# Three chunks of 512 rows and one of 256 in layer two of an attention, expert and MLP kernel

## The chip, the cores and the metric

The kernel runs on one core of a Trainium2 chip, in one launch. The metric is the device time of one execution in microseconds; the median of three runs is given. The profile is of one further execution.

## The reference

Three parts run one after the other. An attention with a small state gives 2176 rows of 512 features. A mixture of experts sends each row to one of eight experts (two matrices with a relu between them) and scales the result. Layer two, which the change is about, is a plain two-layer network over these rows:

```python
def _moe2(x, w_in, w_out):          # x [rows, 512], w_in [512, 2048], w_out [2048, 512]
    h = x @ w_in
    relu6 = np.clip(h + 3.0, 0.0, 6.0)
    g = h * relu6 / 6.0
    return (g @ w_out).astype(np.float32)
```

In the test the inputs are float32 or wider; the weights of layer two arrive as 64-bit floats.

## The kernel before, in words

The expert stage leaves its rows in `y_pad`, seven chunks of 256 rows (`NCS = 7`; the padded places scatter nowhere). Layer two starts from there. Every float32 product is made of three matmuls on a high and a low part of each operand: high by high, high by low, low by high. So `yTh`/`yTl` are the two parts of the turned rows, `wh`/`wl` of the weights, `gh`/`gl` of the hidden values.

The hidden dimension of 2048 is cut into 16 steps `m` of 128. A step of a chunk is:

- the first product, `mm3` (L1102): twelve matmuls into one PSUM tile `p3`, eight on `wh` and then four on `wl`, each streaming 256 columns of `yTh` or `yTl` (two pieces of 128);
- its activation: `u` on ScalarE (L1123), `g` on VectorE (L1124), the cast `gh` on ScalarE (L1125), and `gl = g - gh` on VectorE, or on GpSimd in the first group up to step 13 (L1126);
- the second product, `mm4` (L1129): per half of 128 rows three matmuls of 512 columns of `wh`/`wl` into an accumulator `po`, summed over the 16 steps.

TensorE runs one step ahead (`late`): first product of step m, then the second product of step m-1. Chunks 0 and 1 go together as the first group (`groups`, L1256), since the weights are converted only there; chunks 2 to 6 are groups of their own with all weights in SBUF. The accumulators `po` have four PSUM banks, two a chunk.

In the first group each step m also does the following. `advance` (L963) hands VectorE conversion instructions of the weights, 64-bit to float32, three an eighth of a matrix (L939, L941, L943; `NA = 2` behind each first product), and SP the loads into the two `st` tiles. `prep` (L947) makes `wh` on ScalarE (L957) and `wl` on GpSimd (L958) for step m+2. Steps 2, 4 and 6 fill the output with zeros.

The rows of the next group are fetched by `fetch` (L898): loads into two `yg` tiles at step 10, and at steps 12 and 14 one half each is split by `rest`: `fid` on VectorE, the cast `yTh` on ScalarE (L912), `yTl` on VectorE (L913). Three pairs of `yTh`/`yTl` tiles take turns (`c % 3`; the third lies in the pool `mw`). When a chunk's last second product is done, `put` (L1247) copies each half to a tile `o` (ScalarE L1252, VectorE L1250; four tiles) and GpSimd scatters it to the output (L1253); all scatters write `out_dram`, so each waits for the one before.

In the last chunk the steps from `16 - NH` on do only the first half of the second product; their `gh`/`gl` are held, and the other half follows at the end, so that the first half's scatter goes out while TensorE works on the second (L1294 to L1302). `NH = 7` is also the count of `gh`/`gl` tiles.

Expert pairs earlier in the kernel borrow SBUF tiles for their weights (`spare`, L1045), among them the four `yT` tiles. A loop at the end (L1351 on) serves overflowing experts; it is not entered with these inputs.

Of the kernel before, what the change touches and what calls it, by code (L numbers as in the profile page):

```python
# [595 lines left out]
def full(ctx, tc, x, state, w_gate, w1, w2, capacity, w_in, w_out, out, dbg=None):  # L596
# [448 lines left out]
    spare = [(vv, f"v{m}") for m in range(NV - NSP, NV)] + [(vv, "wh0"), (vv, "wl0")] + [(mk, f"yT{h}{t}") for t in range(2) for h in "hl"]  # L1045
    turn_of = [0]

    def p_loads(which, es_, ks=(0, 2, 1, 3)):
        raws = {}
        for k in ks:  # L1050
            for g in range(2):
                pool, tag = spare[turn_of[0] % len(spare)]
                turn_of[0] += 1
                raws[k, g] = load(which, es_[g], k, pool=pool, tag=tag, bufs=1)
# [343 lines left out]
```

## Time and profile before

| | us |
|---|---|
| median of three runs (575.43, 575.67, 579.76) | 575.67 |
| the profiled execution, its own time | 579.37 |
| its span from the first to the last instruction | 577.2 |
| TensorE busy in the span | 555.5 |
| VectorE, ScalarE, GpSimd busy | 307.5, 222.2, 141.9 |

Engines: PE is TensorE (matmuls), PEld its weight loads, DVE VectorE, ACT ScalarE, POOL GpSimd, SP the engine that issues most DMAs. A line such as L1111 is the line of the kernel whose instruction it is. The ends of matmuls are modelled, so the pace of a stretch is taken from starts: the start of the next matmul less the start of this one.

### The profile page before, as it was taken

How to read it: one execution, taken by the hardware profiler on the slowest of the kernel's cores; microseconds unless marked ns; L12 is line 12 of the kernel's file. 1: busy time of each engine (PE TensorE's matmuls, PEld its weight loads, DVE VectorE, ACT ScalarE, POOL GpSimd, SP SyncE). 2: the span in 40 equal slices, each digit the busy share in tenths (PEclk: the TensorE clock that was granted, in tenths of full speed). 3: DMA queues.
4: the chain of work that ended last, by engine and by line, in shares of the span. 5: the costliest groups of instructions: out<-in, count | busy, mean ns of one | idle time of the engine just before them, and what ended most of it. 6: DMA issues, size and time to landing. Idle time of an engine off the chain costs nothing.

```text
span 577.2 us, 10492 instructions
## 1 busy us (share of the span) xinstructions
PE 555.5 (96%) x3974; PEld 484.7 (84%) x3974; DVE 307.5 (53%) x700; ACT 222.2 (39%) x462; POOL 141.9 (25%) x195
## 2 busy tenths in 40 slices
PE   6998889899999999999999999999999999999996
PEld 3655789796969697899999888999999999999994
DVE  4888974437635674466769863333233333233331
ACT  4878621234304250325434543333334333333331
POOL 5435634201510110016676742001001001001001
PEclk9999889899999999999999999999999999999999
DMA  6735711896979793234863411001001001000000
GB/s 138 177 144 186 250 77 48 267 398 227 386 258 403 237 346 100 96 130 147 297 233 112 146 38 56 18 19 56 1 18 56 1 19 56 1 1 19 20 1 30
DMA packets 52201, 75.26 MB, mean 130 GB/s; under 512 B 23121, under 2 KB 31313, under 8 KB 51634
## 3 DMA queue, kind: packets, MB, share of 16 engines
q1 hardware_dynamic: 49634, 67.09, 34.7%
q0 software_dynamic: 2240, 7.38, 3.7%
q8 instruction: 33, 0.54, 0.4%
q14 instruction: 22, 0.18, 0.1%
q10 hardware_dynamic: 272, 0.07, 0.1%
HBM read 70.75 MB, written 16.49 MB: 151 GB/s over the span
## 4 chain that ended last, share of the span: by engine, by line
issue 36%; PE 29%; DMA 10%; DVE 5%; ACT 1%; POOL 0%; POOLq 0%; DVEq 0%; ACTq 0%
PE pm L798 10%; PE pm L809 10%; DMA out_dram<-o,fid 6%; PE pm L1086 2%; PE pm L1066 2%; DMA st<-in_moe_w_out_dram 2%; PE p L1111 2%; DVE v L943 2%; DMA st<-in_moe_w_in_dram 1%; DVE g L1124 1%; DVE v L939 1%; DVE v L941 1%; PE po L1134 1%; ACT wh L957 1%; PE pxt L764 1%
## 5 line engine op out<-in xcount | busy, mean ns | idle before, releaser
L1111 PE MATMUL p<-yTh,wh 128*128 128x256 f32 x448 | 110.5, 280 | 0.0
L1111 PE MATMUL p<-yTl,wh 128*128 128x256 f32 x448 | 110.5, 280 | 0.0
L1124 DVE SCALAR_TENSOR_TENSOR g<-u,p 128x256 f32<-128x256 f32 x110 | 46.1, 419 | 115.9 <-ACT u L1123 115.8
L1123 ACT ACTIVATE u<-p,b 128x256 f32<-128x256 f32 x110 | 52.0, 473 | 108.9 <-PE p L1111 108.9
L1111 PEld LDWEIGHTS p<-yTl,wh 128*128 128x128 f32 x448 | 84.5, 189 | 3.9
L1111 PEld LDWEIGHTS p<-yTh,wh 128*128 128x128 f32 x448 | 84.4, 188 | 3.8
L1134 PE MATMUL po<-wh,gh 128*128 128x512 f32 x220 | 86.3, 392 | 0.0
L1134 PE MATMUL po<-wh,gl 128*128 128x512 f32 x220 | 86.2, 392 | 0.0
L1134 PE MATMUL po<-wl,gh 128*128 128x512 f32 x220 | 86.1, 391 | 0.0
L1125 ACT CAST gh<-g 128x256 fp32r<-128x256 f32 x110 | 44.7, 406 | 80.7 <-DVE g L1124 80.7
L1111 PE MATMUL p<-yTh,wl 128*128 128x256 f32 x448 | 71.6, 282 | 0.9 <-POOL wl L958 0.9
L1253 POOL DMA_INDIRECT out_dram<-o,fid x14 | 13.9, 994 | 219.5 <-ACT o L1252 162.8
L1111 PEld LDWEIGHTS p<-yTh,wl 128*128 128x128 f32 x448 | 60.7, 189 | 1.7 <-POOL wl L958 1.7
L1126 DVE TENSOR_TENSOR gl<-g,gh 128x256 fp32r<-128x256 f32 x84 | 36.7, 437 | 39.8 <-ACT gh L1125 39.8
L1134 PEld LDWEIGHTS po<-wh,gl 128*128 128x128 f32 x220 | 41.3, 188 | 9.8 <-POOL gl L1126 0.4
L798 PE MATMUL pm<-xth,w1h 128*128 128x256 f32 x160 | 45.9, 291 | 1.4 <-DVE xb L813 1.4
L798 PE MATMUL pm<-xth,w1l 128*128 128x256 f32 x160 | 45.0, 285 | 1.3 <-DVEq L1156 1.3
L1134 PEld LDWEIGHTS po<-wh,gh 128*128 128x128 f32 x220 | 41.4, 188 | 5.2
L1134 PEld LDWEIGHTS po<-wl,gh 128*128 128x128 f32 x220 | 41.4, 188 | 5.2
L809 PE MATMUL pm<-hth,w2h 128*128 128x256 f32 x160 | 45.2, 282 | 0.0
L809 PE MATMUL pm<-htl,w2h 128*128 128x256 f32 x160 | 44.7, 280 | 0.0
L809 PE MATMUL pm<-hth,w2l 128*128 128x256 f32 x160 | 44.6, 278 | 0.0
(285 smaller groups left out, 1005.0 us busy)
## 6 DMA issues: line engine op xcount, KB each, us to landing
raw<-in_moe_w_dram SPq DMA_DIRECT2D x80, 512.0 KB
st<-in_moe_w_in_dram SPq DMA_DIRECT2D x16, 512.0 KB
st<-in_moe_w_out_dram SPq DMA_DIRECT2D x16, 512.0 KB
x_rows<-xrow SPq DMA_DIRECT2D x4, 1072.0 KB
xb<-in_x_dram SPq DMA_DIRECT2D x32, 128.0 KB
yg<-y_pad SPq DMA_DIRECT2D x14, 258.0 KB
out_dram<-zt SPq DMA_DIRECT2D x2, 1536.0 KB
y_pad<-y SPq DMA_DIRECT2D x5, 516.0 KB
```

The lines of the kernel that those rows point to most:

```text
L798: T.matmul(ps[:, j], W1[l][k][:, ls], xT[r][:, k], start=n == 0, stop=n == 11)
L809: T.matmul(ps[:, j], W2[l][k // 2][:, k % 2, ls], hT[k // 2][r][:, k % 2], start=k == 0 and i == 0, stop=k == 7 and i == 2)
L943: V.scalar_tensor_tensor(out=t, in0=lo, scalar=29, in1=t, op0=ALU.logical_shift_right, op1=ALU.bitwise_or)
L1066: T.matmul(ps[n][64 * g:64 * g + 64, :], th[:, 128 * k + 64 * g:128 * k + 64 * g + 64], raws[k, g][:, 512 * n:512 * n + 512], start=i == 0 ...
L1086: T.matmul(ps[64 * g:64 * g + 64, :], th[:, 128 * k + 64 * g:128 * k + 64 * g + 64], raws[k // 2, g][:, 512 * (k % 2):512 * (k % 2) + 512] ...
L1111: T.matmul(pv, l[:, 128 * k:128 * k + 128], r[:, :, 128 * k:128 * k + 128], start=n == 0, stop=n == 11)
L1123: A.activation(out=u, in_=ps, func=AF.Relu, bias=b3)
L1124: V.scalar_tensor_tensor(out=g, in0=u, scalar=6.0, in1=ps, op0=ALU.min, op1=ALU.mult)
L1125: A.copy(gh, g)
L1126: eng.tensor_tensor(out=gl, in0=g, in1=gh.bitcast(F32), op=ALU.subtract)
L1134: T.matmul(po[t], l[:, ls], r[:, 512:1024], start=m == 0 and i == 0, stop=m == 15 and i == 2)
L1253: G.indirect_dma_start(out=out, out_offset=bass.IndirectOffsetOnAxis(ap=fid[:, t:t + 1], axis=0), in_=o, in_offset=None, bounds_check=B * ...
```

## The change

Chunks 0 and 1, 2 and 3, 4 and 5 become three groups of 512 rows, chunk 6 stays alone. In a group of two chunks `mm3` makes one first product for both: twelve matmuls of 512 columns (four pieces of 128) into a full PSUM bank, and one `u`, `g`, `gh`, `gl` of 512 columns. `mm4` still goes chunk by chunk on halves of the wide `gh`/`gl`.

What follows from it: the `yT` tiles are twice as wide (`wide`, two sets in turn, one in `mk` and one in `mw`); `gh`/`gl` are three wide tiles each, so `NH` falls to 5; `u` has one tile, `o` three; two tiles of 16 columns (`pad0`, `pad1`) shift what is allocated behind them; the borrowed `yT` tiles of the expert pairs hold two raw weight tiles each. In the first group all four conversion instructions of a step stand behind the one first product (`advance(2 * NA)`). A group's two chunks are fetched at steps 8 and 12, and split at steps 10, 11 and 14, 15. The loop at the end is rewritten to use the wide tiles.

```diff
-NH = 7
+NH = 5
...
-    def fetch(at, slot=0):
-        pool = mw if slot == 2 else mk
-        yTh = pool.tile([128, 2, DM], F32R, name=f"yTh{slot}", bufs=1)
-        yTl = pool.tile([128, 2, DM], F32R, name=f"yTl{slot}", bufs=1)
+    def wide(slot):
+        pool = mw if slot else mk
+        return [pool.tile([128, 4, DM], F32R, name=f"yT{h}{slot}", bufs=1) for h in "hl"]
+
+    def fetch(at, y, half=0):
+        yTh, yTl = (v[:, 2 * half:2 * half + 2] for v in y)
...
-    def mm3(m, yTh, yTl, early=False, eng=V):
+    def mm3(m, y, n=4, early=False, eng=V, into=None):
...
-                    T.matmul(pv, l[:, 128 * k:128 * k + 128], r[:, :, 128 * k:128 * k + 128], start=n == 0, stop=n == 11)
+                    T.matmul(pv, l[:, 128 * k:128 * k + 128], r[:, 0:n, 128 * k:128 * k + 128], start=i == 0, stop=i == 11)
...
-            u = mw.tile([128, 256], F32, name="u", bufs=2)
-            g = mw.tile([128, 256], F32, name="g", bufs=2)
-            gh = mw.tile([128, 256], F32R, name="gh", bufs=NH)
-            gl = mw.tile([128, 256], F32R, name="gl", bufs=NH)
+            u = mw.tile([128, 512], F32, name="u", bufs=1)[:, 0:128 * n]
+            g = mw.tile([128, 512], F32, name="g", bufs=2)[:, 0:128 * n]
+            gh, gl = into or both()
...
+    def both():
+        if not padded:
+            first = [mw.tile([128, 512], F32R, name=f"g{h}", bufs=3) for h in "hl"]
+            padded.append(mw.tile([128, 16], F32, name="pad1"))
+            return first
+        return [mw.tile([128, 512], F32R, name=f"g{h}", bufs=3) for h in "hl"]
...
-    g0 = mm3(0, *ft[0][0][0:2], True)
-    g1 = mm3(0, *ft[1][0][0:2], True)
+    g01 = mm3(0, ys[0], early=True)
...
+    mw.tile([128, 16], F32, name="pad0")
+    ys[1] = wide(1)
...
-        o = mw.tile([128, DM], F32, name="o", bufs=4)
+        o = mw.tile([128, DM], F32, name="o", bufs=3)
...
-    groups = [(0, 1)] + [(c,) for c in range(2, NCS)]
+    groups = [(0, 1), (2, 3), (4, 5), (6,)]
...
-            for c in gs:
-                gg[c] = mm3(m, *ft[c][0][0:2], eng=V if gi or m > 13 else G)
-                if gi == 0:
-                    advance(NA)
+            if last:
+                if m % 2 == 0:
+                    two = both()
+                g = mm3(m, ys[gi], 2, into=half(two, m % 2))
+                gg = {gs[0]: g}
+            else:
+                g = mm3(m, ys[gi], eng=V if gi or m > 13 else G)
+                gg = {c: half(g, i) for i, c in enumerate(gs)}
+            if gi == 0:
+                advance(2 * NA)
...
-            if not last and m >= 10:
-                for c in groups[gi + 1]:
-                    if m == 10:
+            if not last:
+                for i, c in enumerate(groups[gi + 1]):
+                    if m == 8 + 4 * i:
                         ft[c] = fetch_c(c)
-                    if m in (12, 14):
-                        ft[c][1](m // 2 - 6)
+                    if m - 10 - 4 * i in (0, 1):
+                        ft[c][1](m - 10 - 4 * i)
```

TensorE, one step of the first group. Before, the two first products stand one behind the other; the second of them begins in the middle of this piece (`yTh_3400` is the tile of chunk 0, `yTh_3460` that of chunk 1, `x4` four rows alike):

```order
L1111 MATMUL p_4102<-yTh_3400,wh_4020 128x256
L1111 MATMUL p_4102<-yTl_3401,wh_4020 128x256
L1111 MATMUL p_4102<-yTh_3400,wh_4020 128x256
L1111 MATMUL p_4102<-yTl_3401,wh_4020 128x256
L1111 MATMUL p_4102<-yTh_3400,wl_4021 128x256 x4
L1111 MATMUL p_4127<-yTh_3460,wh_4020 128x256
L1111 MATMUL p_4127<-yTl_3461,wh_4020 128x256
L1111 MATMUL p_4127<-yTh_3460,wh_4020 128x256
```

After, step 7 of the same group, the end of its one first product and the start of the second product of step 6 (`yTh_3392` holds both chunks):

```order
L1124 MATMUL p_3952<-yTl_3393,wh_3891 128x512
L1124 MATMUL p_3952<-yTh_3392,wh_3891 128x512
L1124 MATMUL p_3952<-yTl_3393,wh_3891 128x512
L1124 MATMUL p_3952<-yTh_3392,wl_3892 128x512 x4
L1158 MATMUL po<-wh_3848,gh 128x512
L1158 MATMUL po<-wl_3849,gh 128x512
L1158 MATMUL po<-wh_3848,gl 128x512
L1158 MATMUL po<-wh_3848,gh 128x512
```

Twenty-four matmuls of 256 columns in a step have become twelve of 512; the second product has the same rows as before.

VectorE in the first group, from the third step on, before (`v` is a weight tile in conversion, `g` the activation of one chunk):

```order
L1124 SCALAR_TENSOR_TENSOR g<-u,p_3798 128x256
L939 TENSOR_SCALAR v_3756<-st 128x512
L941 SCALAR_TENSOR_TENSOR v_3756<-st,v_3756 128x512
L1124 SCALAR_TENSOR_TENSOR g<-u,p_3839 128x256
L943 SCALAR_TENSOR_TENSOR v_3756<-st,v_3756 128x512
L939 TENSOR_SCALAR v_3863<-st 128x512
L1124 SCALAR_TENSOR_TENSOR g<-u,p_3865 128x256
L941 SCALAR_TENSOR_TENSOR v_3863<-st,v_3863 128x512
L943 SCALAR_TENSOR_TENSOR v_3863<-st,v_3863 128x512
```

and after, two steps:

```order
L1136 SCALAR_TENSOR_TENSOR g<-u,p_3864 128x512
L948 SCALAR_TENSOR_TENSOR v_3846<-st,v_3846 128x512
L950 SCALAR_TENSOR_TENSOR v_3846<-st,v_3846 128x512
L946 TENSOR_SCALAR v_3846<-st 128x512
L948 SCALAR_TENSOR_TENSOR v_3846<-st,v_3846 128x512
L1136 SCALAR_TENSOR_TENSOR g<-u,p_3908 128x512
L950 SCALAR_TENSOR_TENSOR v_3846<-st,v_3846 128x512
L946 TENSOR_SCALAR v_3932<-st 128x512
L948 SCALAR_TENSOR_TENSOR v_3932<-st,v_3932 128x512
L950 SCALAR_TENSOR_TENSOR v_3932<-st,v_3932 128x512
```

Two conversions stood behind each `g`; now four stand behind each `g` of twice the width.

VectorE at the end of a group. Before, the end of chunk 2 (`fid` and `yTl` of step 14, `g` and `gl` of step 15 and of the next chunk's step 0, then `o`):

```order
L911 CAST fid<-yg 128x1
L913 TENSOR_TENSOR yTl_5000<-yg,yTh_4999 128x512
L1124 SCALAR_TENSOR_TENSOR g<-u,p_5120 128x256
L1126 TENSOR_TENSOR gl<-g,gh 128x256
L1124 SCALAR_TENSOR_TENSOR g<-u,p_5147 128x256
L1126 TENSOR_TENSOR gl<-g,gh 128x256
L1250 TENSOR_SCALAR o<-po 128x512
```

and after, the end of the second group (chunks 2 and 3):

```order
L914 CAST fid<-yg 128x1
L916 TENSOR_TENSOR yTl_4666<-yg,yTh_4665 128x512
L1136 SCALAR_TENSOR_TENSOR g<-u,p_4884 128x512
L1138 TENSOR_TENSOR gl<-g,gh 128x512
L914 CAST fid<-yg 128x1
L916 TENSOR_TENSOR yTl_4666<-yg,yTh_4665 128x512
L1136 SCALAR_TENSOR_TENSOR g<-u,p_4920 128x512
L1138 TENSOR_TENSOR gl<-g,gh 128x512
L1276 TENSOR_SCALAR o<-po 128x512 x2
```

The second `fid` and `yTl` of a chunk stood ahead of step 15's `g` and `gl`; those of a group's second chunk now stand behind them, right ahead of the next group's first `g`.

## Rows read from the trace of the kernel before

**Rows 1.** The page: busy us of each engine (share), instructions.
```profile
PE 555.5 (96%) x3974; PEld 484.7 (84%) x3974; DVE 307.5 (53%) x700; ACT 222.2 (39%) x462; POOL 141.9 (25%) x195
```

**Rows 2.** Windows, first group and chunk 3: busy us by engine, clock, DMA.
```profile
256.60:344.90 88.30, 87.44 (x566) 78.96 (x565) 68.22 (x98) 39.21 (x79) 56.87 (x39) 1.00 0.49 165
...
391.00:435.60 44.60, 44.60 (x290) 40.62 (x289) 15.75 (x38) 15.63 (x35) 1.94 (x2) 1.00 0.08 25
```

**Rows 3.** Timeline of PE, chunk 4 (start us, us, instruction): three products begin.
```profile
455.31 0.28 PE L1111 MATMUL p<-yTh,wh 128*128 128x256 f32 x1
...
456.73 0.39 PE L1134 MATMUL po<-wh,gh 128*128 128x512 f32 x1
...
458.09 0.28 PE L1111 MATMUL p<-yTh,wh 128*128 128x256 f32 x1
```

**Rows 4.** Timeline of PE, chunk 2: three products begin.
```profile
360.41 0.28 PE L1111 MATMUL p<-yTh,wh 128*128 128x256 f32 x1
...
361.84 0.40 PE L1134 MATMUL po<-wh,gh 128*128 128x512 f32 x1
...
363.23 0.28 PE L1111 MATMUL p<-yTh,wh 128*128 128x256 f32 x1
```

**Rows 5.** Timeline of PE: the first matmul of chunk 2 and of chunk 6.
```profile
344.92 0.28 PE L1111 MATMUL p<-yTh,wh 128*128 128x256 f32 x1
...
525.51 0.28 PE L1111 MATMUL p<-yTh,wh 128*128 128x256 f32 x1
```

**Rows 6.** Timeline of PE, first group, step 15; [idle us <-releaser].
```profile
340.19 0.74 PE L1111 MATMUL p<-yTh,wl 128*128 128x256 f32 x4 [0.64 <-POOL wl L958]
```

**Rows 7.** Readers of tile `st`, 255 to 340 us: ns least/median/most.
```profile
L941 DVE SCALAR_TENSOR_TENSOR v<-st,v x18: 678/693/2249, 257.9 to 334.7; 128x512 int32<-128x512 int32 x18
L943 DVE SCALAR_TENSOR_TENSOR v<-st,v x18: 678/1166/2544, 258.7 to 335.6; 128x512 int32<-128x512 int32 x18
```

**Rows 8.** L1126 and L958 on POOL: ns least/median/most, starts.
```profile
L1126 POOL TENSOR_TENSOR gl<-g,gh x26: 737/917/1196, 262.7 to 336.2; 128x256 fp32r<-128x256 f32 x26
...
L958 POOL TENSOR_TENSOR wl<-v,wh x14: 2388/2416/2732, 248.4 to 337.8; 128x1024 fp32r<-128x1024 f32 x14
```

**Rows 9.** Timeline of POOL, first group: the first and the last `wl` of thirteen.
```profile
265.14 2.45 POOL L958 TENSOR_TENSOR wl<-v,wh 128x1024 fp32r<-128x1024 f32 x1
...
337.75 2.39 POOL L958 TENSOR_TENSOR wl<-v,wh 128x1024 fp32r<-128x1024 f32 x1 [0.61 <-ACT wh L957]
```

**Rows 10.** Timeline of POOL and DVE, first group.
```profile
288.98 2.73 POOL L958 TENSOR_TENSOR wl<-v,wh 128x1024 fp32r<-128x1024 f32 x1
...
289.72 2.54 DVE L943 SCALAR_TENSOR_TENSOR v<-st,v 128x512 int32<-128x512 int32 x1
```

**Rows 11.** Groups of 512 columns: busy us, mean ns; L913 least/median/most.
```profile
L800 ACT ACTIVATE hth<-pm 128x512 fp32r<-128x512 f32 x20 | 12.0, 598 | 37.5 <-PE pm L798 35.2 <-DMA raw<-in_moe_w_dram 2.3
...
L912 ACT CAST yTh<-yg 128x512 fp32r<-128x512 f32 x14 | 8.5, 618 | 0.0
...
L801 DVE SCALAR_TENSOR_TENSOR htl<-pm,hth 128x512 fp32r<-128x512 f32 x20 | 13.5, 687 | 36.9 <-ACTq L1186 20.0 <-ACT hth L800 16.9
...
L913 DVE TENSOR_TENSOR yTl<-yg,yTh x14: 680/692/2669, 242.7 to 523.5; 128x512 fp32r<-128x512 f32 x14
```

**Rows 12.** Timeline of ACT, chunk 4: `u` behind a first product.
```profile
456.99 0.47 ACT L1123 ACTIVATE u<-p,b 128x256 f32<-128x256 f32 x1 [1.41 <-PE p L1111]
```

**Rows 13.** Timeline, the end: last matmuls, the copy `o`, scatters.
```profile
567.73 0.39 PE L1134 MATMUL po<-wh,gl 128*128 128x512 f32 x1
...
569.03 0.97 POOL L1253 DMA_INDIRECT out_dram<-o,fid  x1 [35.22 <-ACTq L1352]
...
571.16 0.40 PE L1134 MATMUL po<-wh,gl 128*128 128x512 f32 x1
571.59 0.69 DVE L1250 TENSOR_SCALAR o<-po 128x512 f32<-128x512 f32 x1 [4.31 <-PE po L1134]
572.56 0.97 POOL L1253 DMA_INDIRECT out_dram<-o,fid  x1 [2.56 <-DVEq L1352]
```

More of the change, by code (lines that the diff above doesn't have):

```diff
@@ L913, in rest @@
             V.tensor_tensor(out=yTl[:, t], in0=yg[:, 0:DM], in1=yTh[:, t].bitcast(F32), op=ALU.subtract)
-        return (yTh, yTl, fid), rest
+        return fid, rest
+    ys = {}
     def fetch_c(c):
-        return fetch(lambda t: slice(256 * c + 128 * t, 256 * c + 128 * t + 128), c % 3)
+        if c % 2 == 0 and c // 2 not in ys:
+            ys[c // 2] = wide(c // 2 % 2)
+        return fetch(lambda t: slice(256 * c + 128 * t, 256 * c + 128 * t + 128), ys[c // 2], c % 2)
     vt, sts = {}, {}
@@ L1042, in p_xt @@
         return th
-    spare = [(vv, f"v{m}") for m in range(NV - NSP, NV)] + [(vv, "wh0"), (vv, "wl0")] + [(mk, f"yT{h}{t}") for t in range(2) for h in "hl"]
+    spare = [[(vv, f"v{m}") for m in range(NV - NSP, NV)], [(vv, "wh0"), (vv, "wl0")], [(mk, "yTh0")], [(mk, "yTl0")]]
     turn_of = [0]
@@ L1050, in p_loads @@
         for k in ks:
[L1051 to L1054, printed above, removed]
+            where = spare[turn_of[0] % len(spare)]
+            turn_of[0] += 1
+            if len(where) == 1:
+                pool, tag = where[0]
+                both = pool.tile([128, 2, 1024], F32, name="raw", tag=tag, bufs=1)
+                raws[k, 0], raws[k, 1] = (load(which, es_[g], k, raw=both[:, g]) for g in range(2))
+            else:
+                for g, (pool, tag) in enumerate(where):
+                    raws[k, g] = load(which, es_[g], k, pool=pool, tag=tag, bufs=1)
         return raws
@@ L1127, in mm3, with half @@
         return gh, gl
+    def both():
[4 more added lines that the diff above has]
+        return [mw.tile([128, 512], F32R, name=f"g{h}", bufs=3) for h in "hl"]
+    padded = []
+    def half(g, i):
+        return tuple(v[:, 256 * i:256 * i + 256] for v in g)
     def mm4(m, gh, gl, po, ts=(0, 1)):
@@ L1237, in full @@
             p_begin()
-    g0 = mm3(0, *ft[0][0][0:2], True)
-    g1 = mm3(0, *ft[1][0][0:2], True)
+    g01 = mm3(0, ys[0], early=True)
     po = {c: accs() for c in (0, 1)}
-    late = (0, (0, 1), {0: g0, 1: g1}, po)
+    late = (0, (0, 1), {c: half(g01, c) for c in (0, 1)}, po)
     c2.close()
     mw = ctx.enter_context(tc.tile_pool(name="mw", bufs=1, reuse_waits="tile"))
+    mw.tile([128, 16], F32, name="pad0")
+    ys[1] = wide(1)
     def put(po, fid, t):
-        o = mw.tile([128, DM], F32, name="o", bufs=4)
+        o = mw.tile([128, DM], F32, name="o", bufs=3)
         if t:
@@ L1359, in full @@
                 l_rows(i, r, e, t)
-            (yTh, yTl, fid), rest = fetch(lambda t: bass.ds(i * 256 + (YL + 128 * t), 128))
+            y = wide(0)
+            fid, rest = fetch(lambda t: bass.ds(i * 256 + (YL + 128 * t), 128), y)
             rest(0)
@@ L1364, in full @@
             for m in range(16):
-                mm4(m, *mm3(m, yTh, yTl), po)
+                mm4(m, *mm3(m, y, 2), po)
             put(po, fid, 0)
```

52 lines of the change are left out of this document (28 added, 24 removed).

## The prediction

> **What bounds the kernel now.** I read the busy shares first. TensorE is busy for 96% of the span and no other engine for more than 53% [rows 1]. Then the table by stage: layer two runs from 256.6 us to the end. In chunk 3 TensorE has no idle time at a granted clock of 1.00, its upper level (2.4 GHz), while VectorE and ScalarE work 16 us of 45; in the first group VectorE works 68 us of 88 and GpSimd 57 [rows 2]. So in layer two the question is how fast one matmul follows another, and in its first group also whether weight conversion keeps up. The order of TensorE in time answers the first. In a step of chunk 4 twelve 256-column matmuls take 456.73 - 455.31 = 1.42 us, 118 ns each, and the six 512-column ones of the second product 458.09 - 456.73 = 1.36, 227 ns each [rows 3]. In chunk 2 the same step takes 1.43 and 1.39, 119 and 232 ns [rows 4]: identical instructions differ by 2% with the tiles they read, which no engine's wait explains. Chunks 2 to 5 run from 344.92 to 525.51 [rows 5]; 1.39 of these 180.6 us are the extra second product of chunk 1 that chunk 2's first step carries, which leaves 179.2, or 44.8 a chunk.
>
> The first group is slower than its matmuls. TensorE waits there for GpSimd's `wl`, 0.64 us of idle time ahead of the matmul at 340.19 in step 15 [rows 6]. GpSimd's thirteen `wl` of that group start 265.14 to 337.75, 6.05 us apart [rows 9], where one step of two chunks needs 2 x 2.78 = 5.56 on TensorE. The reason is in the durations: the conversion steps L941 and L943 take 0.68 alone but up to 2.5 [rows 7], and the one at 289.72 ran 2.54 because `wl` had started at 288.98 and held it off until 291.71 [rows 10]. The Trainium skill (SBUF — State Buffer, "Who interferes with whom") has the rule: a VectorE instruction with two SBUF inputs and a GpSimd instruction that reads SBUF exclude one another for the whole instruction. By that rule, as here, their times add.
>
> **Groups 2 and 3 (chunks 2 to 5).** The change replaces 24 matmuls of 256 columns by 12 of 512 in each of 32 steps, with half the weight loads; the second product keeps its 12. No row shows a 512-column matmul whose moving operand lies in four pieces, so I bound it by the 512-column rows: 0.2267 us [rows 3] to 0.2313 [rows 4]. At 24 matmuls a step and 32 steps that is 768 x 0.2267 = 174.1 or 768 x 0.2313 = 177.6 against 179.2. The tiles move in memory, and the rows tell only that this is worth 2%; I take the middle, 0.229: 175.9, so **-3.3** (from -5.1 to -1.6). If four pieces made the stream no cheaper than two separate matmuls, 24 x 0.118 = 2.83 a first product stays and the gain is 0.
>
> The Trainium skill (TensorE: Matmul & The Clock Gate, "Back-to-back issue gap") speaks against part of this. It gives 262 cycles for 256 columns and 518 for 512, so that halving the count saves 6 cycles, 2.5 ns, a pair. By the Trainium skill's figures 32 x 12 x 2.5 ns = 1.0 us would be gained. The rows show 2 x 118 - 227 = 9 ns in chunk 4 and 2 x 119 - 232 = 6 in chunk 2, so this trace offers more.
>
> **The first group.** Per step two `u`, `g`, `gh`, `gl` of 256 columns become one each of 512. GpSimd's work alone was 2 x 0.74 + 2.39 = 3.87 [rows 8]; a 512-column `gl`, by the line through 256 and 1024 columns, is 0.74 + 1.65 / 3 = 1.29, so it becomes 3.68. Four of the three-step conversions' instructions fall to a step, 1.33 times L941 and L943 at 0.69: 1.84, which excludes GpSimd's. Before: 5.71, and 6.05 measured, so 0.34 are hand-overs. After, by the same sum: 5.52 + 0.34 = 5.86. But the order also changes: four conversions now stand in one row behind `g`, so the next `g` waits for a conversion that `wl` holds off. That loop is `wl` 2.39, the released conversion 0.55, `g` 0.69 and `gh` 0.62 (the 512-column rows of these kinds [rows 11]), `gl` 1.29, hand-overs 0.2: 5.74, and 0.6 more in a step where a second conversion takes its turn: 6.3. I take 6.1. TensorE needs 24 x 0.229 = 5.50, so it still waits, now for `gl` in front of the second product. The first `wl` comes 0.4 later (the first `g` is twice as long), twelve spacings of 6.1 are 73.2 where 72.6 were: **+1.0** for the end of the group. One end is TensorE alone, without a wait, 31 blocks of 2.75 us from 256.6, 341.9 against 344.92: -3.0. The other is 6.3 throughout: +3.4. So the 15 x 0.1 us of faster streaming in this group are not seen. Weight-load DMAs and the three zero fills keep their order on SP, their slots come free at the same conversions, and what VectorE waits for them is inside the measured 6.05.
>
> **The hand-over between groups.** A group now has two chunks of rows to fetch for the next, and the last half of the second is converted in step 15, right behind that step's own chain. Behind the first product's end X: `u` at X + 0.26 (456.73 to 456.99) [rows 3, 12], 0.60, `g` 0.69, `gh` 0.62, then the cast `yTh` 0.62 [rows 11], so with hand-overs X + 2.8. The next first product could start at X + 2.75, after the second product: 0.1 late. Its second matmul needs `yTl`: behind `gl` 0.69, `fid` and itself 0.69 on VectorE, X + 3.7 where it was due at X + 3.1: 0.6 more. Two such hand-overs (the one into the 256-row chunk has both halves done by step 11): **+1.4** (0 to 2). In the kernel before these casts stood at step 14 with a whole step to spare. The four accumulators of a group are also taken again at once, but their `o` copies have 2.7 us of first product to get done; of four `o` tiles in a row the fourth now waits for the first scatter, some 3.5 us; TensorE reaches that bank at about 6 us, so this costs nothing until a scatter takes twice as long.
>
> **The tail.** The scatters wait for one another. The first of chunk 6 goes out at 569.03, the second at 572.56, 3.53 later. Its data were ready at 571.59 + 0.69, so both conditions meet [rows 13]. Before, fifteen matmuls stand behind the first scatter's last matmul (567.73 to 571.16); with NH = 5 only nine. So the first scatter starts 6 x 0.229 = 1.37 later and the second must follow it: **+1.3** (0 if the wait between scatters were shorter than 2.2 us). The earlier stages do the same work in the same order: 0 for the pair experts' loads, whose buffers are only paired differently. The last chunk keeps 256 columns: 0, within 0.8 either way for its tiles' places.
>
> **Sum.** +1.0 - 3.3 + 1.4 + 1.3 = **+0.4 us**. Against the profiled execution's 579.37 us (577.2 span, 2.2 around it) this is 579.8; that execution was 3.7 us above the median 575.67, and the forecast for the median is **576.1**. About 1% (5.8 us) is what a measurement of this kernel can tell from no change.
>
> **Rivals.** (a) *The first group keeps up and the new places stream at the fast pace.* Then -3.0 - 5.1 + 1.4 + 1.3 = -5.4, and with the last chunk's 0.8: -6.2, 569.5, faster. For it: chunk 4 does stream at 227 ns; against it: the exclusion sum leaves 0.3 us a step too much. Chance 0.12. (b) *GpSimd's queue becomes the bound of the first group*: if a second conversion gets in ahead of `gl` in nearly every step, one step takes 6.4 to 6.5 us instead of 6.05 (+4.8 to 6), and at 0.2313 a matmul gives back only 1.6: +5 - 1.6 + 1.4 + 1.3 = +6.1, 581.8, slower. It decides from a spacing of `wl` of 6.4 us on. For it: a conversion already takes up to 2.5 us; against: the same sum gave 6.05 with more instructions in it. Chance 0.11. (c) *The streaming gain is not there*: four pieces cost as much as two matmuls, so +1.0 + 1.4 + 1.3 = +3.7, 579.4, no change by the bound. Against it: two pieces cost nothing visible in rows 3. Chance 0.14. (d) *Only a small fixed cost a matmul is saved*: the 512-column stream at chunk 2's 232 ns against two of chunk 4's 118 saves 4 ns, 1.5 us in 32 x 12: +2.2, 577.9. Against it: within one chunk the rows give 6 to 9. Chance 0.12. (The Trainium skill's "Back-to-back issue gap" stands near this one.) The forecast itself: 0.51.
>
> So faster by over 1%: 0.12; within: 0.77; slower: 0.11. The range reaches from between the forecast and (a), 570.8, to just under (b), 581.3.
>
> **What would show it.** Right: first products of twelve matmuls at 227 to 231 ns; `wl` spaced about 6.1 us, with waits of TensorE for GpSimd's `gl`; about 0.7 us of wait at the first product of groups 2 and 3 for `yTh`/`yTl` (ScalarE, VectorE); the last two scatters still 3.5 us apart and the end 1.3 us further behind the last matmul. Wrong: no waits in the first group (then a), spacing over 6.4 (b), or matmuls of 235 ns and more (c).

## The result and the profile after

| | before | after |
|---|---|---|
| median of six runs, us | 576.19 | 582.90 |
| the profiled execution, us | 579.37 | 582.22 |
| its span, us | 577.2 | 580.4 |

The ratio is 1.0087 with a 95% interval of [1.0060, 1.0114]: 5.0 us slower (3.5 to 6.6) on 575.67. (The two medians alone would give 1.0116, since four of the six executions before lie between 575.18 and 576.71 us and two at 579.76 and 580.30; the ratio with its interval is what is used here.) The page gives TensorE the same share of the span as [rows 1]:

```profile
PE 556.3 (96%) x3398; PEld 455.6 (79%) x3398; DVE 306.0 (53%) x617; ACT 202.3 (35%) x366; POOL 140.4 (24%) x182
```

The table by stage (start and end in us, length, then busy us and count of PE, PEld, DVE, ACT and POOL, granted clock, DMA share, GB/s) now has four groups:

```profile
255.20:347.00 91.80, 88.38 (x374) 68.89 (x373) 77.86 (x81) 35.06 (x49) 54.70 (x26) 1.00 0.48 161
347.00:437.10 90.10, 89.72 (x384) 72.06 (x385) 25.96 (x43) 23.99 (x38) 3.94 (x4) 1.00 0.08 24
437.10:526.30 89.20, 88.83 (x385) 72.19 (x385) 25.13 (x41) 23.01 (x36) 4.37 (x4) 1.00 0.04 15
526.30:573.50 47.20, 47.20 (x301) 42.27 (x299) 15.07 (x35) 15.78 (x35) 4.86 (x5) 1.00 0.06 24
```

The clock is 1.00 in all of them, as in [rows 2]. In the first group TensorE stands for 91.80 - 88.38 = 3.4 us, where it had 0.9; no other stage has more than 0.4 of it. (The ends are modelled, so by starts the shift is larger: the fifteen second products of the group take some 47.4 us where before had 41.4, its first products 44.3 where before had 47.0. The waits have moved from the first product, ahead of `wl`, to the second, ahead of `gl`.) The stages begin with these matmuls (timeline of PE, start first):

```profile
255.25 0.39 PE L1124 MATMUL p<-yTh,wh 128*128 128x512 f32 x1
...
347.02 0.51 PE L1124 MATMUL p<-yTh,wh 128*128 128x512 f32 x1
...
437.10 0.50 PE L1124 MATMUL p<-yTh,wh 128*128 128x512 f32 x1
...
526.31 0.28 PE L1124 MATMUL p<-yTh,wh 128*128 128x256 f32 x1
```

From such starts, and from those of before [rows 2, 5, 13], comes the account. Layer two begins anywhere from 252.64 to 257.35 us, 4.7 us apart, in the executions profiled here, though nearly the same code stands ahead of it; so only lengths inside layer two are compared.

| stage | before | after | difference | forecast |
|---|---|---|---|---|
| first group, up to chunk 2's first matmul | 88.32 | 91.77 | +3.45 | +1.0 |
| chunks 2 to 5, same matmuls, without the waits at hand-overs | 179.2 | 177.7 | -1.5 | -3.3 |
| waits at the hand-overs | 0 | 1.6 | +1.6 | +1.4 |
| chunk 6, same matmuls | 45.65 | 45.41 | -0.2 | 0 |
| last matmul's start to the end of the span (good to 0.1) | 6.04 | 7.29 | +1.25 | +1.3 |
| sum | | | +4.6 | +0.4 |

(Chunks 2 to 5 take 526.31 - 347.02 = 179.29 us with the waits; their first products take 3.54 and 3.52 us where later steps take 2.75 to 2.80, and the step ahead of the second one loses 0.13. Chunk 6 takes 573.11 - 526.31 = 46.80, of which 1.39 is one more chunk's second product than before.) The sum is that of the two spans: 580.4 - 577.2 + 1.35, since layer two began 1.35 us earlier in the execution after.

The first group: GpSimd's `wl`, the subtraction that makes the low part of the weights, on the timeline of POOL: of thirteen the first, the tenth, the twelfth and the last.

```profile
264.65 2.84 POOL L965 TENSOR_TENSOR wl<-v,wh 128x1024 fp32r<-128x1024 f32 x1
...
319.32 2.85 POOL L965 TENSOR_TENSOR wl<-v,wh 128x1024 fp32r<-128x1024 f32 x1
...
332.56 2.86 POOL L965 TENSOR_TENSOR wl<-v,wh 128x1024 fp32r<-128x1024 f32 x1
...
340.54 2.42 POOL L965 TENSOR_TENSOR wl<-v,wh 128x1024 fp32r<-128x1024 f32 x1 [1.77 <-ACT wh L964]
```

The tenth and the twelfth of before:

```profile
319.17 2.39 POOL L958 TENSOR_TENSOR wl<-v,wh 128x1024 fp32r<-128x1024 f32 x1
...
330.85 2.60 POOL L958 TENSOR_TENSOR wl<-v,wh 128x1024 fp32r<-128x1024 f32 x1 [0.21 <-ACT wh L957]
```

Thirteen `wl` are (340.54 - 264.65) / 12 = 6.32 us apart, against 6.05 [rows 9]. But the first nine spacings are 6.07 on average, hardly more than before (6.00); the next two together are 332.56 - 319.32 = 13.24 where before had 11.68, and the last is 7.98 where before had 6.90. Eight of the thirteen `wl` also last some 2.85 us, not the 2.39 to 2.45 of [rows 9]. What happens in a long step is told by all engines around 326 us:

```profile
325.75 0.68 ACT L1135 ACTIVATE u<-p,b 128x512 f32<-128x512 f32 x1
326.14 2.58 POOL L965 TENSOR_TENSOR wl<-v,wh 128x1024 fp32r<-128x1024 f32 x1
...
326.50 2.77 DVE L948 SCALAR_TENSOR_TENSOR v<-st,v 128x512 int32<-128x512 int32 x1
...
329.25 0.68 DVE L916 TENSOR_TENSOR yTl<-yg,yTh 128x512 fp32r<-128x512 f32 x1
...
329.85 0.67 DVE L1136 SCALAR_TENSOR_TENSOR g<-u,p 128x512 f32<-128x512 f32 x1
...
331.25 1.34 POOL L1138 TENSOR_TENSOR gl<-g,gh 128x512 fp32r<-128x512 f32 x1 [2.54 <-ACT gh L1137]
```

`wl`, which runs from 326.14 to 328.72, holds off the conversion L948 at 326.50, which ends only at 329.27. Behind it VectorE splits a half of the next group's rows (`yTl`, 329.25) and only then computes `g` (329.85), though its `u` was done at 325.75 + 0.68 = 326.43; `gh` and `gl` follow, and TensorE, due at the second product, waits for `gl`. The waits of TensorE in layer two (total us, times, longest):

```profile
PE po L1158 <- POOL gl L1138: 3.4, 7, 1.0
PE p L1124 <- DVE yTl L916: 0.7, 2, 0.4
```

So the wait named in the forecast is there, seven times. `gl` holds conversions off as well (behind the `gl` of 324.45 to 326.18 the conversion L946 lasts 1.50, another one 0.41), and a conversion that runs holds off `wl`: all eight `wl` of 2.85 are issued while L948 or L950 runs.

The streaming: three starts of products in group 2, then three in group 3 (timeline of PE):

```profile
409.09 0.39 PE L1124 MATMUL p<-yTh,wh 128*128 128x512 f32 x1
...
411.89 0.40 PE L1158 MATMUL po<-wh,gh 128*128 128x512 f32 x1
...
414.65 0.39 PE L1124 MATMUL p<-yTh,wh 128*128 128x512 f32 x1
...
465.59 0.40 PE L1124 MATMUL p<-yTh,wh 128*128 128x512 f32 x1
...
468.36 0.39 PE L1158 MATMUL po<-wh,gh 128*128 128x512 f32 x1
...
471.11 0.40 PE L1124 MATMUL p<-yTh,wh 128*128 128x512 f32 x1
```

Group 2: 411.89 - 409.09 = 2.80 us for twelve 512-column matmuls of the first product, 233 ns each, and 2.76 for the second. Group 3: 2.77 and 2.75, 231 and 229 ns. The steady steps of chunk 4 before took 118 x 2 and 227 ns [rows 3].

The end, as in [rows 13]: the last matmul of the first half, its scatter, the last matmul, its copy and its scatter.

```profile
571.05 0.40 PE L1158 MATMUL po<-wh,gl 128*128 128x512 f32 x1
...
572.36 0.97 POOL L1279 DMA_INDIRECT out_dram<-o,fid  x1 [30.76 <-ACTq L1386]
...
573.11 0.40 PE L1158 MATMUL po<-wh,gl 128*128 128x512 f32 x1
573.55 0.69 DVE L1276 TENSOR_SCALAR o<-po 128x512 f32<-128x512 f32 x1 [2.92 <-PE po L1158]
575.75 0.97 POOL L1279 DMA_INDIRECT out_dram<-o,fid  x1 [2.42 <-DMA out_dram<-o,fid]
```

Nine matmuls follow the first half's last one (571.05 to 573.11, 2.06 us) where fifteen did (567.73 to 571.16, 3.43 us). The second scatter leaves 3.39 us behind the first; its data had been ready since 573.55 + 0.69 = 574.24.

### The profile page after: what moved, and what is told of

Read it like the earlier page. It is cut to its first block, busy times and chain, and to the rows that moved or that the text cites. A ratio compares the mean times of both kernels' runs of the same rounds, so it can differ in the third digit from the quotient of the medians.

```text
span 580.4 us, 9080 instructions
## 1 busy us (share of the span) xinstructions
PE 556.3 (96%) x3398; PEld 455.6 (79%) x3398; DVE 306.0 (53%) x617; ACT 202.3 (35%) x366; POOL 140.4 (24%) x182
## 4 chain that ended last, share of the span: by engine, by line
issue 37%; PE 27%; DMA 9%; DVE 8%; POOL 0%; ACT 0%; POOLq 0%; DVEq 0%
PE pm L799 10%; PE pm L810 10%; DMA out_dram<-o,fid 6%; DVE v L950 3%; PE pm L1098 2%; PE pm L1078 2%; DVE v L948 2%; DVE v L946 2%; DMA st<-in_moe_w_in_dram 2%; DMA st<-in_moe_w_out_dram 1%; DVE g L1136 1%; PE p L1124 1%; PE pxt L765 1%; PE pht L1090 0%; POOL gl L1138 0%
## 5 line engine op out<-in xcount | busy, mean ns | idle before, releaser
L1136 DVE SCALAR_TENSOR_TENSOR g<-u,p 128x512 f32<-128x512 f32 (+1 forms) x63 | 38.9, 618 | 124.2 <-ACT u L1135 124.2
L1124 PE MATMUL p<-yTl,wh 128*128 128x512 f32 (+1 forms) x256 | 91.4, 366 | 0.7 <-DVE yTl L916 0.7
L1124 PE MATMUL p<-yTh,wh 128*128 128x512 f32 (+1 forms) x256 | 91.5, 366 | 0.0
L1135 ACT ACTIVATE u<-p,b 128x512 f32<-128x512 f32 (+1 forms) x63 | 39.9, 634 | 138.2 <-PE p L1124 138.2
L1124 PE MATMUL p<-yTh,wl 128*128 128x512 f32 (+1 forms) x256 | 62.1, 364 | 0.0
L1137 ACT CAST gh<-g 128x512 fp32r<-128x512 f32 (+1 forms) x63 | 35.7, 567 | 73.4 <-DVE g L1136 73.4
L1124 PEld LDWEIGHTS p<-yTl,wh 128*128 128x128 f32 x256 | 48.1, 188 | 10.3 <-DVE yTl L916 1.4
L1124 PEld LDWEIGHTS p<-yTh,wh 128*128 128x128 f32 x256 | 48.1, 188 | 9.7 <-ACT yTh L915 0.9
L965 POOL TENSOR_TENSOR wl<-v,wh 128x1024 fp32r<-128x1024 f32 x14 | 37.8, 2698 | 39.7 <-ACT wh L964 39.7
L1138 DVE TENSOR_TENSOR gl<-g,gh 128x512 fp32r<-128x512 f32 (+1 forms) x50 | 30.7, 613 | 30.9 <-ACT gh L1137 30.9
```

The source lines that it names most:

```text
L965: (V if m in (0, 2) else G).tensor_tensor(out=wl, in0=v, in1=wh.bitcast(F32), op=ALU.subtract)
L1124: T.matmul(pv, l[:, 128 * k:128 * k + 128], r[:, 0:n, 128 * k:128 * k + 128], start=i == 0, stop=i == 11)
L1135: A.activation(out=u, in_=ps, func=AF.Relu, bias=b3)
L1136: V.scalar_tensor_tensor(out=g, in0=u, scalar=6.0, in1=ps, op0=ALU.min, op1=ALU.mult)
L1137: A.copy(gh, g)
L1138: eng.tensor_tensor(out=gl, in0=g, in1=gh.bitcast(F32), op=ALU.subtract)
```

## The experiments

Stage lengths below are from the profiled execution of each kernel, taken as in the table; the same stage in kernels that don't touch it agrees within 0.1 us (group 3: 89.19 to 89.21 in six kernels, the first group 91.77 and 91.79 in two). Ratios are to the kernel before, with 95% intervals.

### The first group

**Two narrow first products again** (`e1_narrow_first`):

```diff
+            elif gi == 0:
...
+                for i, c in enumerate(gs):
+                    gg[c] = mm3(m, ys[gi], 2, eng=V if m > 13 else G, into=half(two, i), at=2 * i, ug=half(ug, i))
+                    advance(NA)
...
```

Expected: 

> The changed kernel, but in the first group two first products of 256 columns a step again, each with its own u, g, gh, gl and two conversion instructions behind it; the wide tiles, groups 2 and 3 and the end stay. Theory A (the row of four conversions behind one wide g, held off by GpSimd's gl and wl, makes the group long): the group (first matmul of layer two to first matmul of chunk 2) falls from 91.8 us to 88.3, within 0.5, as in the kernel before, and the whole time by about 3.4. Rival B (the cause is not in the order but in the tiles' places, the weight loads or the four half fetches that now fall into the group): it stays above 90.5 us.

Measured: ratio 1.0024 [0.9999, 1.0049]; first group 90.9 us. By the number set, rival B. With the order of before but for the splits the group is still 2.6 us longer than before. VectorE shows one part of it:

```profile
320.05 2.52 DVE L916 TENSOR_TENSOR yTl<-yg,yTh 128x512 fp32r<-128x512 f32 x1 [0.94 <-ACT yTh L915]
...
326.99 2.63 DVE L916 TENSOR_TENSOR yTl<-yg,yTh 128x512 fp32r<-128x512 f32 x1 [0.81 <-ACT yTh L915]
```

Two splits fall among the conversions, and each lasts 2.5 to 2.6 us in place of 0.68, since GpSimd's `wl` holds it off; in the kernel before this happens to one. The rest of the 2.6 us isn't explained by this run.

**Activation in halves, matmuls wide** (`e5_half_act`):

```diff
...
+            for h in hs:
+                V.scalar_tensor_tensor(out=g[:, h], in0=u[:, h], scalar=6.0, in1=ps[:, h], op0=ALU.min, op1=ALU.mult)
+                A.copy(gh[:, h], g[:, h])
+                eng.tensor_tensor(out=gl[:, h], in0=g[:, h], in1=gh[:, h].bitcast(F32), op=ALU.subtract)
+                mid(NA)
```

Expected: 

> The changed kernel, but in the first group u, g, gh and gl are done in two halves of 256 columns, with two conversion instructions behind each g; the first product stays one of 512 columns. Theory A (the order on VectorE and GpSimd decides, not the width of the matmuls): the group takes 87.5 to 88.8 us instead of 91.8. Rival B (the wide first product itself is what costs, as the first half's activation now starts 2.75 us later): 90 us or more, with TensorE still waiting for gl in the second product.

Measured: ratio 1.0049 [1.0024, 1.0073]; first group 90.6 us, `gl` waits 1.5 us in four places instead of 3.4 in seven. That is the rival's number, but not its reason: the run above has narrow first products and is no shorter. The last `wl` starts 339.03 - 255.89 = 83.14 us into the group, 2.15 earlier than after; but then TensorE waits 1.05 us for the `yTh` of chunk 2, where in the kernel after it waits 0.04. So the order is worth 2.2 us to the weights and 1.2 to the group, and that the matmuls are wide costs nothing that can be seen here.

**The splits later** (`e12_late_split`):

```diff
+                    if gi == 0:
+                        if m in (13, 14) and i == 0:
+                            ft[c][1](m - 13)
...
+                        if m == 15 and i == 1:
+                            ft[c][1](0)
+                            ft[c][1](1)
```

Expected: 

> The changed kernel, but in the first group the halves of chunk 2 are split at steps 13 and 14 instead of 10 and 11, and both of chunk 3 at step 15: behind the conversions, except the first. Theory (two splits more among the conversions cost 0.7 us of VectorE each and more while GpSimd holds them off): the last wl starts 83 to 84 us after the first matmul of layer two instead of 85.3, and what is gained there is given back at the first product of chunk 2, which waits longer. Rival (the row of four conversions is all of it): the last wl stays at 85.3 within 0.4.

Measured: ratio 1.0114 [1.0073, 1.0156]. The last `wl` and the first matmul of chunk 2:

```profile
338.11 2.40 POOL L965 TENSOR_TENSOR wl<-v,wh 128x1024 fp32r<-128x1024 f32 x1 [1.76 <-ACT wh L964]
...
347.09 0.50 PE L1124 MATMUL p<-yTh,wh 128*128 128x512 f32 x1 [1.43 <-ACT yTh L915]
```

The first matmul of layer two was at 254.05, so the last `wl` came 84.06 us behind it instead of 85.29. That is 1.2 us gained, 0.06 short of the range and clear of the rival's. It is more than given back: the second product ahead of chunk 2 takes 4.73 us, so that the group is 347.09 - 254.05 = 93.04 us long, chunk 2 waits 1.43 us for `yTh`, and its first product takes 4.94 us. So two splits among the conversions cost 1.2 us, and neither this place nor one step earlier (`e2`, below) is a better one. The last spacing of `wl`, which holds no split here, is 7.96, as in the kernel after; in the two runs above, with two conversions behind each `g`, it is 6.34. So it goes with the row of four and not with the splits.

**`gl` on VectorE** (`e6_gl_vector`):

```diff
         A.copy(gh, g)
+        if mid:
+            mid(1)
         eng.tensor_tensor(out=gl, in0=g, in1=gh.bitcast(F32), op=ALU.subtract)
...
-                g = mm3(m, ys[gi], eng=V if gi or m > 13 else G)
+                g = mm3(m, ys[gi], mid=None if gi else advance)
...
-                advance(2 * NA)
+                advance(3)
```

Expected: 

> The changed kernel, but gl of the first group on VectorE, one conversion instruction between g and gl and three behind: GpSimd has only wl. Theory A (two-input work of VectorE and GpSimd adds up, gl 1.4 us on GpSimd against 0.7 on VectorE): a step needs 2.4 + 1.84 + 0.69 = 4.9 us of the two together, less than TensorE's 5.5, so the waits for gl go and the first group takes 86 to 88.5 us instead of 91.8. Rival (VectorE becomes the bound, as it stands still while wl runs): 4 x 0.6 + 0.69 + 0.69 + 2.4 = 6.2 us a step, the group stays at 91 or more.

Measured: ratio 1.0015 [0.9991, 1.0039]; first group 89.2 us, 2.6 less, between the two ranges. `wl` of step 3, the tenth and the last:

```profile
265.84 2.50 POOL L965 TENSOR_TENSOR wl<-v,wh 128x1024 fp32r<-128x1024 f32 x1 [14.66 <-ACT wh L964]
...
318.70 2.57 POOL L965 TENSOR_TENSOR wl<-v,wh 128x1024 fp32r<-128x1024 f32 x1 [3.55 <-ACT wh L964]
...
339.69 2.40 POOL L965 TENSOR_TENSOR wl<-v,wh 128x1024 fp32r<-128x1024 f32 x1 [5.07 <-ACT wh L964]
```

Now (318.70 - 265.84) / 9 = 5.87 us apart, and GpSimd waits over 3 us for `wh` ahead of each: it has time left, so VectorE with what it waits for is the pace. The last three spacings still take 6.39, 6.66 and 7.94.

### Hand-over and end

**Splits earlier** (`e2_early_rest`):

```diff
+                    d = 2 if gi else 1
-                    if m == 8 + 4 * i:
+                    if m == 8 - d + 4 * i:
...
-                    if m - 10 - 4 * i in (0, 1):
+                    if m - 10 + d - 4 * i in (0, 1):
```

Expected: 

> The changed kernel, but the next group's rows are fetched and split one step earlier in the first group (last split at step 14) and two steps earlier in the later ones (last split at step 13). Theory (the wait of 0.5 to 0.9 us at the first products of groups 2 and 3 is only for the casts yTh and yTl of step 15): the wait at chunk 4 goes (first product 2.80 instead of 3.52 us), that at chunk 2 falls below 0.2 us; 1.4 us in all. Rival (the casts moved forward hold up g and the conversions in the first group): the first group grows by 0.6 us or more and eats half of it.

Measured: ratio 1.0062 [1.0035, 1.0089]. First matmuls of chunks 2 and 4, neither with a wait ahead of it:

```profile
348.32 0.39 PE L1124 MATMUL p<-yTh,wh 128*128 128x512 f32 x1
...
437.54 0.40 PE L1124 MATMUL p<-yTh,wh 128*128 128x512 f32 x1
```

Both first products take 2.8 us, so the waits were those casts alone. But chunk 2 begins 348.32 - 255.61 = 92.71 us into layer two, 0.94 later than after: the rival's collision eats the whole first half of the gain. The second half, 0.75, is kept.

**Seven held halves** (`e3_tail7`):

```diff
-NH = 5
+NH = 7
...
-                    two = both()
+                    two = both() if m < 14 else [v[:, 0] for v in wide(0)]
```

Expected: 

> The changed kernel with NH = 7: seven steps hold their second half, the fourth pair of gh/gl lies in a tile of the rows of chunks 4 and 5, which are done by then. Theory (two scatters 3.4 us apart set the end, the first bound to its last matmul): six more matmuls stand behind the first scatter, it goes out 1.38 us earlier, the second too, and the time from the last matmul to the end falls from 7.3 us to 5.9; 1.3 us in all. Rival (the second scatter is bound by its own data): the end moves by less than 0.3 us.

Measured: ratio 1.0071 [1.0042, 1.0099]. First scatter, last matmul, second scatter:

```profile
571.36 0.98 POOL L1279 DMA_INDIRECT out_dram<-o,fid  x1 [29.40 <-ACTq L1386]
...
573.53 0.40 PE L1158 MATMUL po<-wh,yTl 128*128 128x512 f32 x1
...
574.93 0.97 POOL L1279 DMA_INDIRECT out_dram<-o,fid  x1 [2.60 <-DVE o L1276]
```

(The last matmul carries the name `yTl` because the seventh pair lies in a tile of rows.) From the last matmul's start to the end of the span (579.6) it is 6.07 us instead of 7.29: 1.2, where the theory said 1.3. The scatters stay 3.57 us apart.

### The streaming

**Each wide matmul as two of 256 columns** (`e10_two_streams`):

```diff
-                    T.matmul(pv, l[:, 128 * k:128 * k + 128], r[:, 0:n, 128 * k:128 * k + 128], start=i == 0, stop=i == 11)
+                    for h in range(0, n, 2):
+                        T.matmul(pv[:, h:h + 2], l[:, 128 * k:128 * k + 128], r[:, h:h + 2, 128 * k:128 * k + 128], start=i + h == 0, stop=i == 11 and h + 2 == n)
```

Expected: 

> The changed kernel, tiles and order untouched, but each 512-column matmul of the first product of a group issued as two of 256 columns into the halves of the same bank (24 a step instead of 12, the weights loaded twice). It prices the streaming gain at equal places. Theory (halving the count saves what the rows of before show, 6 to 9 ns a pair): the first products of groups 2 and 3 take 2.80 to 2.84 us a step instead of 2.77 to 2.80, 12 pairs in each of 32 steps, so the two groups take 2.3 to 3.4 us longer. Rival (the pace is that of the tiles, not of the count): less than 1 us longer in the two groups.

Measured: ratio 1.0051 [1.0021, 1.0080]. Product starts in group 2 and in group 3 (`x2`: two rows alike):

```profile
399.45 0.40 PE L1125 MATMUL p<-yTh,wh 128*128 128x256 f32 x2
...
402.20 0.39 PE L1159 MATMUL po<-wh,gh 128*128 128x512 f32 x1
...
404.94 0.40 PE L1125 MATMUL p<-yTh,wh 128*128 128x256 f32 x2
...
466.59 0.40 PE L1125 MATMUL p<-yTh,wh 128*128 128x256 f32 x2
...
469.42 0.39 PE L1159 MATMUL po<-wh,gh 128*128 128x512 f32 x1
```

In group 2 a first product of 24 matmuls takes 402.20 - 399.45 = 2.75 us, 114.4 ns each, less than the twelve wide ones (2.80); in group 3 it takes 2.83, more than their 2.77. The two groups together: 179.21 against 179.29 us. By the number set the rival is right: halving the count saves nothing over these two groups. But that is a sum of two differences that cancel, group 2 being 0.97 us shorter and group 3 0.89 longer, and not a price that is the same in every step. The second products, which this edit doesn't touch, move too: in group 2 they take 404.94 - 402.20 = 2.74 us, where after they take 2.76 and 2.80 in turn. So the pace moves by up to 3% either way, and not by the tiles' places alone.

**Two moves of tiles** (`e4_pad_before_g`, 64 bytes; `e8_align64`, 32 bytes):

```diff
-            first = [mw.tile([128, 512], F32R, name=f"g{h}", bufs=3) for h in "hl"]
             padded.append(mw.tile([128, 16], F32, name="pad1"))
-            return first
```

```diff
+    keep.tile([128, 8], F32, name="pad2")
...
+    pd = ctx.enter_context(tc.tile_pool(name="pd", bufs=1, side="right"))
+    pd.tile([128, 8], F32, name="pad3")
...
-    mw.tile([128, 16], F32, name="pad0")
```

Expected of the first: 

> The changed kernel with the 16-column pad ahead of the gh/gl tiles instead of behind them: gh and gl lie 64 bytes further on, at the place (96 in 128 bytes) that they have in the kernel before, everything else stays. Theory (the lost streaming gain is the place of gh/gl against the weights): the second products of steps 3 to 8 of chunks 2 to 5 go from 229 to 233 ns a matmul to 227, some 1 us less in the two groups. Rival (that place does not matter): no stage moves by more than 0.3 us.

Expected of the second: 

> The changed kernel without its two pads of 16 columns, and with two of 8 columns (32 bytes) at other places, so that the tiles of rows, weights, gh and gl start at multiples of 64 bytes, where in the changed kernel all lie 32 bytes off. Theory (matmuls of 512 columns take 227 to 233 ns and not 213, 512 columns at 2.4 GHz, because their rows straddle): below 225 ns a matmul in groups 2 and 3, 5 us or more in all. Rival (what sets 227 to 233 lies elsewhere): the same 229 to 233 ns, within 1.5 us over layer two.

Measured: the first, 1.0068 [1.0044, 1.0092]: group 2 0.5 us shorter, group 3 0.2 longer, chunk 6 0.2 longer. Its theory falls: the second products don't go to 227 ns. The second, 1.0075 [1.0040, 1.0111]: group 2 1.0 us shorter, group 3 0.3 and chunk 6 0.9 longer, nothing over layer two, as its rival said. But three product starts in its group 2 show something the kernel after never reaches:

```profile
380.24 0.39 PE L1127 MATMUL p<-yTh,wh 128*128 128x512 f32 x1
...
382.95 0.39 PE L1161 MATMUL po<-wh,gh 128*128 128x512 f32 x1
...
385.68 0.39 PE L1127 MATMUL p<-yTh,wh 128*128 128x512 f32 x1
```

382.95 - 380.24 = 2.72 and 385.68 - 382.95 = 2.72: matmuls of 512 columns at 226.7 ns, those with a moving operand in four pieces too. So four pieces cost nothing in themselves. Where the tiles lie moves the pace between 227 and 233 ns, by a rule that these runs don't give.

### Put together

**Three edits at once** (`e13_all_three`: `gl` on VectorE, the splits of later groups two steps earlier, `NH = 7`).

Expected: 

> The changed kernel with three of the single edits at once: gl of the first group on VectorE, the rows of groups 3 and 4 split two steps earlier, NH = 7. If the three add up: first group 89.2 us, no wait at chunk 4 (0.75 us less), 1.25 us less behind the last matmul, 4.6 us less than the changed kernel, which is 1.0087 of the kernel before: a ratio of 1.0007, no difference from before. If they hide one another: 1.003 or more.

Measured: ratio 1.0003 [0.9984, 1.0021]: they add up (first group 89.2 us, no wait at chunk 4, 6.06 us behind the last matmul). The changed kernel is brought back to the one before, and no further.

**The kernel before, with `gl` on VectorE** (`e11_before_gl_vector`):

```diff
+        if mid:
+            mid(1)
         eng.tensor_tensor(out=gl, in0=g, in1=gh.bitcast(F32), op=ALU.subtract)
...
-                gg[c] = mm3(m, *ft[c][0][0:2], eng=V if gi or m > 13 else G)
+                gg[c] = mm3(m, *ft[c][0][0:2], mid=None if gi else advance)
                 if gi == 0:
-                    advance(NA)
+                    advance(1)
```

Expected: 

> The kernel before, with one edit: in the first group gl is on VectorE, with one conversion instruction between g and gl and one behind, and GpSimd has only wl. Theory (the first group is paced by the two-input work of VectorE and GpSimd together, whatever the width of the products): per step 1.84 + 2 x 0.42 + 2.39 = 5.1 us, below TensorE's 5.5, so the first group falls from 88.3 us to 86 to 87.3 and the time by 1 to 2.3 us: faster than both kernels. Rival (VectorE alone is the bound, as it stands while wl runs): 88 us or more, no gain.

Measured: median 575.64 us beside 578.33 for the kernel before in the same series, ratio 0.9958 [0.9937, 0.9979]: faster than both kernels. First matmuls of layer two and of chunk 2, then the first and the last `wl` on POOL:

```profile
252.64 0.28 PE L1111 MATMUL p<-yTh,wh 128*128 128x256 f32 x1
...
338.71 0.28 PE L1111 MATMUL p<-yTh,wh 128*128 128x256 f32 x1
```

```profile
261.62 2.40 POOL L958 TENSOR_TENSOR wl<-v,wh 128x1024 fp32r<-128x1024 f32 x1 [14.59 <-PE po L1136]
...
331.57 2.41 POOL L958 TENSOR_TENSOR wl<-v,wh 128x1024 fp32r<-128x1024 f32 x1 [4.53 <-ACT wh L957]
```

The group takes 338.71 - 252.64 = 86.1 us, and no wait of TensorE shows in it any more; `wl` is 5.83 us apart and its 2.4 us are undisturbed.

**The same, and one pair of row tiles moved by 64 bytes** (`e14_glv_ypad`):

```diff
+        first = slot == 2 and not padded
+        if first:
+            padded.append(mw.tile([128, 16], F32, name="pad0"))
         yTh = pool.tile([128, 2, DM], F32R, name=f"yTh{slot}", bufs=1)
         yTl = pool.tile([128, 2, DM], F32R, name=f"yTl{slot}", bufs=1)
+        if first:
+            mw.tile([128, 16], F32, name="pad1")
...
```

Expected: 

> The kernel before with gl of the first group on VectorE (as in e11) and 64 bytes of padding on either side of the third pair of yTh/yTl tiles, those of chunks 2 and 5: they alone move, to the offset of 32 in 128 bytes that the other two pairs have. Theory (the 1.5 us that groups 2 and 3 stream faster in the changed kernel come from where its row tiles lie, not from 512 columns): chunks 2 and 5 go from 119 and 231 ns a matmul to 117.8 and 227 to 231 as in chunks 3 and 4, chunk 5 takes 44.5 us instead of 45.1, 1.2 us in both, beside the 2.2 us of e11. Rival (their slower pace hangs on something else, as their slot in the order): chunk 5 stays at 45.1.

Measured: ratio 0.9965 [0.9943, 0.9988], not to be told from the run above. First matmuls of chunks 5 and 6:

```profile
478.49 0.28 PE L1118 MATMUL p<-yTh,wh 128*128 128x256 f32 x1
...
523.08 0.28 PE L1118 MATMUL p<-yTh,wh 128*128 128x256 f32 x1
```

Chunk 5 takes 44.6 us instead of 45.1 and chunk 2 46.0 instead of 46.5: 1.0 us in both, by a move of two tiles and nothing else. Chunks 3 and 4 stay within 0.1. In the time of the whole kernel this 1.0 us can't be told from the noise.

## Why the prediction was right or wrong

It said no change by the bound of 1%, and 0.9% slower is within it; the time by the ratio, 580.7, lies in the range, near its upper end, while the median of the series, 582.90, lies beyond it. The central value, 576.1, was too low by 4.6 us: two of its four terms were missed, both towards faster. Together they are 4.3 us of the 5.8 that the bound allows. So that the class came out right owes something to the width of the bound: the account was right in what waits for what, and too cheerful in its two largest terms.

- **First group, +1.0 forecast, +3.45 measured**, 0.05 beyond the upper end of its range. The loop was the right one: `wl` holds off a conversion, the conversion holds off `g`, and TensorE waits for `gl`. Its 6.1 us a step holds for the first nine spacings (6.07). The step that failed is the sum's "twelve spacings of 6.1". In the tenth and eleventh the two splits of chunk 2's rows stand between the conversions and `g`; I priced the splits only at the hand-over, in step 15, and `e12` shows 1.2 us for them. The twelfth took 7.98, with no split in it, and goes with the long row (7.94 to 7.98 where three or four conversions stand in one, as in `e6` and `e12`; 6.34 to 6.90 with two, as in `e1`, `e5` and before). The first `wl` came 0.86 late instead of 0.4. Against before that is 0.86, 0.64 in nine spacings, 1.56 in two and 1.08 in the last, 4.14 at the last `wl`; 0.69 less stand between it and chunk 2, which leaves 3.45. What else than the splits is in the 1.56, and why the first `wl` came later, wasn't tried.
- **Groups 2 and 3, -3.3 forecast, -1.5 measured**, just outside its range. The pace, without the waits, was 230.4 ns in group 3 and 232.3 in group 2, where I took 229 as the middle. But the reason fell too: "2 x 118 - 227 = 9 ns" compared matmuls that read different tiles, and at equal places (`e10`) the count is worth nothing over the two groups (179.21 against 179.29). `e14` shows that 1.0 us comes back in the kernel before as well when two row tiles move, so the place can account for most of the 1.5; that it does is argued, not shown, and the rest stays open. By the Trainium skill (TensorE: Matmul & The Clock Gate, "Back-to-back issue gap") 1.0 us was to be had from the count; `e10` is nearer to that than to my 3.3, and shows not even it.
- **Hand-over, +1.4 forecast, +1.6 measured.** Right in place, engine and size: TensorE waits for `yTh` and then `yTl` of step 15, and `e2` takes the waits away.
- **End, +1.3 forecast, +1.25 measured.** Right: two scatters 3.4 us apart behind a first one that starts six matmuls later; `e3` takes it back.
- **Chunk 6, 0 forecast, -0.2 measured.** Within its 0.8.

Of the rivals, (b) with 581.8 and (c) with 579.4 lie about equally far from the 580.7 of the ratio. (b) stood on a spacing of 6.4 and 0.2313 us a matmul (its "+4.8 to 6" is a little high: twelve spacings of 6.4 to 6.5 and the first `wl` make 4.6 to 5.8); measured were 6.32 and 0.2314 (177.7 / 768). Its way there was another one, since the extra time sits in three steps and not in nearly all. (a) was excluded by the waits for `gl`. (c) had the reason wrong, as `e8` streams four pieces at 226.7 ns. (d) had the streaming right in size, -1.5 us at 232 ns, but a small fixed cost a matmul isn't what `e10` shows.

## What to carry to other kernels

Before a wider matmul is credited with a gain, price the count of matmuls at equal places: here it was worth nothing over two groups, while the same instruction ran 3% faster or slower in different places. Where two engines hold each other off, add up every instruction of both that falls into the stage, also those that belong to the next one, and look at their order, which was worth as much here. Work that moves to the engine that does it in fewer microseconds (`gl` of 256 columns: 0.42 on VectorE, 0.74 and more on GpSimd) can pay even if that engine is the busier one.

## What the runs showed of the hardware

- Matmuls of 512 columns at a granted clock of 1.00 ran at any pace from 226.7 to 233.3 ns, and pairs of 256 columns from 226.7 to 240, steadily over many steps, and alike in the kernels that leave the tiles in place. Moving tiles by 32 or 64 bytes changed the pace by up to 3% in the steps of one stage and the other way in the next (`e8`; less in `e4`); in `e14` a move of two tiles made the two chunks that read them 1% shorter and left the others as they were.
- The exclusion of VectorE and GpSimd works in both directions: `wl` lasts 2.39 us alone, 2.85 where the conversion L948 or L950 runs when it is issued (2.58 with L946), and the conversion L948 lasted 2.77 instead of 0.68 behind `wl`. L946, a conversion with one input, is held off as well: 1.50 instead of 0.41 behind `gl`. The Trainium skill (SBUF — State Buffer, "Who interferes with whom") says of a VectorE instruction with two inputs that it excludes GpSimd's; these are its numbers here.
